# Fused attention kernel: computing 58 of 1184 softmax score banks with VectorE and GpSimd instead of ScalarE

## The chip, the cores and the metric

One NeuronCore of a Trainium2 chip runs the kernel. Times are device microseconds (us) of whole executions. Engines: PE (matmul), PEld (its weight loads), ACT (ScalarE), DVE (VectorE), POOL (GpSimd), SP (SyncE, here only a DMA queue). A ratio is the mean time of one kernel's fast runs over that of the kernel before in the same rounds, so it is not quite the ratio of the medians quoted beside it. One execution of the kernel before was slow (636 us, granted clock 0.655) and is in no ratio.

## The reference

Two attentions over 2048 tokens, model width 448, 16 heads of 28, bf16. Cut to what matters:

```python
# A: plain attention
scores = einsum('bhqd,bhkd->bhqk', q, k) * Dh ** -0.5
o = einsum('bhqk,bhkd->bhqd', softmax(scores), v)          # then @ wo
# B: four segments of 512: masked attention within a segment,
# mixed with a linear-attention memory of the earlier segments
o = g * (phi(qs) @ M) / (phi(qs) @ z + 1e-6) + (1 - g) * (softmax(logits + mask) @ vs)
M = M + phi(ks).T @ vs; z = z + phi(ks).sum()
```

## The kernel before

The work is cut into "banks" of 128 keys x 512 queries of one head. Three banks form a unit: PE writes its scores into one PSUM tile, and one ScalarE instruction takes the exp of all three. PE multiplies the weights with the values two units later. A "query block" is 512 queries of four heads of A (64 banks, 21.3 units). There are 16 of these; eight smaller "B blocks" are put between the later ones.

```python
ps = scp.tile([P, NB, CW], FP32, tag="sc", name="ps_s")        # two buffers of 3 banks
short = min(WARM - state["cols"] - P * nmask, 2 * CW) if u > 0 else 0
...                                                            # filler matmuls on `warm`
pt = ptp.tile([P, NB, CW], BF16, tag="pt", name="pt")
nc.scalar.activation(out=pt[:, 0:n, :], in_=ps[:, 0:n, :], func=ACT.Exp, scale=scale)
```

All other work (projections, outputs, B's memory) is "filler". PE does some columns of it in each unit. Every filler that multiplies writes one of the two PSUM buffers of the "ring" and DVE evicts it; the value accumulators `acc` use the same ring. When a query block ends, its denominators make a trip through DRAM, timed in units after the end:

```python
nc.vector.tensor_copy(out=o[:, 0, :], in_=a[:])                # evict acc
nc.sync.dma_start(out=d1..., in_=o[DH:P:HP, 0:planes, :])      # denominators out
at(u + 3, step1)    # SP:  load them back, spread over partitions
at(u + 7, step2)    # DVE: reciprocal;  SP: out again
at(u + 9, step3)    # SP:  load them broadcast
at(u + 14, step4)   # DVE: multiply
at(u + 16, step5)   # release the output projections as fillers
```

`loadB` (a filler) issues six weight loads and 16 transposing loads. At `nu - 2` (two units before the end) all fillers that are left run at once.

The softmax here doesn't subtract the row's maximum and nothing guards it: scores larger than these inputs give would overflow.

## Time and profile before

Median 581.53 us of 4 runs (580.49 to 585.9).

The page's busy table, then the page's costliest group. Columns of the group: line, engine, operation, output and input, shapes, count; busy us and mean ns of one; idle time of the engine just before them and what ended it.

```profile
PE 525.7 (91%) x3916; PEld 172.5 (30%) x3916; DVE 197.6 (34%) x388; ACT 548.7 (95%) x427; POOL 21.3 (4%) x41
...
L452 ACT ACTIVATE pt<-ps_s 128x1536 bf16<-128x1536 f32 x395 | 538.2, 1583 | 11.5 <-PE ps_s L439 5.9
```

The busy time of each engine between the start of the first exp and the end of the last (columns: stretch, its length, busy time of each engine with instruction counts, granted PE clock, DMA share, GB/s):

```profile
12.90:568.53 555.63, 510.80 (x3840) 165.22 (x3840) 191.60 (x370) 544.47 (x420) 14.45 (x27) 1.00 0.15 38
```

ScalarE idles for 555.63 - 544.47 = 11.2 us of that stretch. PE looks as busy, but 367 of its matmuls are filler on the warm tile. ScalarE is what bounds the kernel.

### The profile page before, as it was taken

To read this page: it belongs to the slowest core of one execution; us is meant where nothing else is said; L and a number is where in the kernel's file an instruction comes from. 1 tells how busy PE (TensorE), PEld (TensorE's weight loads), DVE (VectorE), ACT (ScalarE), POOL (GpSimd) and SP (SyncE) were. 2 spreads that over 40 slices of the span, in tenths; PEclk is the share of its full clock that TensorE was granted. 3 is DMA by queue.
4 is the path that set the end of the run, shared out by engine and by line. 5 is a ranking of instruction groups with operands and counts; after the bars stand their busy time and mean duration, and the time that the engine had idled before them with its cause. 6 is when DMAs were issued, how large, how long until landed. Compare 5 with 4: busy or idle time off the path is not lost.

```text
span 579.1 us, 9661 instructions
## 1 busy us (share of the span) xinstructions
PE 525.7 (91%) x3916; PEld 172.5 (30%) x3916; DVE 197.6 (34%) x388; ACT 548.7 (95%) x427; POOL 21.3 (4%) x41
## 2 busy tenths in 40 slices
PE   7999999999998998899899989989998998889985
PEld 3333322222232322332233322322322323323322
DVE  1232323222223323344434231324344354364212
ACT  3999999999999999999999999999999999999982
POOL 5700000000000000000000000000000000000000
PEclk9999999999999999999999999999999999999999
DMA  7600000001630000002002011021040121142101
GB/s 190 112 1 22 2 20 1 21 0 45 144 68 15 21 1 20 1 3 75 4 9 73 2 29 53 3 68 36 5 120 17 23 77 35 27 135 75 59 17 48
DMA packets 43571, 24.26 MB, mean 42 GB/s; under 512 B 31180, under 2 KB 37164, under 8 KB 43528
## 3 DMA queue, kind: packets, MB, share of 16 engines
q1 hardware_dynamic: 41784, 21.22, 14.5%
q10 hardware_dynamic: 1248, 1.53, 0.9%
q0 software_dynamic: 496, 0.91, 0.7%
q8 instruction: 30, 0.49, 0.4%
q14 instruction: 13, 0.11, 0.1%
HBM read 15.60 MB, written 4.37 MB: 34 GB/s over the span
## 4 chain that ended last, share of the span: by engine, by line
ACT 59%; PE 21%; issue 14%; DVE 3%; DMA 2%; SPq 0%; POOL 0%; ACTq 0%; DVEq 0%; POOLq 0%
ACT pt L452 56%; PE ps_s L439 5%; PE acc L484 4%; PE ps_proj L171 3%; PE ps_s L430 2%; PE ps_s L448 2%; PE ps_y L595 1%; ACT phq L508 1%; DMA w<-in_A_wqkv_dram 1%; ACT ek L691 1%; DVE y L603 1%; DVE osb L539 1%; PE ps_mem L520 1%; PE ps_v L199 1%; DMA bc<-d 0%
## 5 line engine op out<-in xcount | busy, mean ns | idle before, releaser
L452 ACT ACTIVATE pt<-ps_s 128x1536 bf16<-128x1536 f32 x395 | 538.2, 1583 | 11.5 <-PE ps_s L439 5.9
L439 PE MATMUL ps_s<-qTA,kTA 32*128 32x512 bf16 x1024 | 135.3, 384 | 2.1 <-ACT pt L452 1.5
L430 PE MATMUL ps_s<-warm,ident 128*128 128x512 bf16 (+6 forms) x367 | 101.7, 330 | 32.9 <-ACT pt L452 24.9
L484 PE MATMUL acc<-pt,vA 128*32 128x512 bf16 x1024 | 128.4, 390 | 0.2 <-DVE vA L188 0.2
L439 PEld LDWEIGHTS <-kTA 32*128 32x128 bf16 x1024 | 34.8, 90 | 143.5 <-issue 141.6
L484 PEld LDWEIGHTS <-vA 128*32 128x32 bf16 x1024 | 32.3, 92 | 70.7 <-issue 68.8
L430 PEld LDWEIGHTS <-ident 128*128 128x128 bf16 x367 | 35.3, 97 | 53.2 <-issue 43.7
L539 DVE COPY osb<-acc 128x512 f32<-128x512 f32 x32 | 22.1, 692 | 57.4 <-PE acc L484 57.1
L603 DVE CAST y<-ps_y 128x448 bf16<-128x448 f32 x28 | 17.5, 624 | 50.6 <-PE ps_y L595 50.6
L448 PE MATMUL ps_s<-tri,negi 128*128 128x128 bf16 x256 | 25.0, 222 | 0.0
L439 PE MATMUL ps_s<-qTB,kTB 32*128 32x384 bf16 (+3 forms) x256 | 24.5, 301 | 0.1
L176 DVE CAST kTA<-ps_proj 128x512 bf16<-128x512 f32 x15 | 10.4, 692 | 37.4 <-PE ps_proj L171 37.4
L176 DVE CAST qTA<-ps_proj 128x512 bf16<-128x512 f32 x15 | 10.4, 691 | 33.5 <-PE ps_proj L171 33.5
L171 PE MATMUL ps_proj<-xTB,wpqB 128*128 128x512 bf16 x64 | 20.7, 385 | 1.1 <-DVE macc L715 0.8
L171 PE MATMUL ps_proj<-xTB,wpkB 128*128 128x512 bf16 x64 | 20.6, 384 | 0.5
L204 DVE CAST vB<-ps_v 128x448 bf16<-128x448 f32 x16 | 9.9, 620 | 29.5 <-PE ps_v L199 29.5
L171 PE MATMUL ps_proj<-xTA,wpkA 128*128 128x512 bf16 x60 | 19.3, 384 | 0.5
L171 PE MATMUL ps_proj<-xTA,wpqA 128*128 128x512 bf16 x60 | 18.9, 384 | 0.8
L176 DVE CAST kTB<-ps_proj 128x512 bf16<-128x512 f32 x16 | 10.9, 684 | 24.1 <-PE ps_proj L171 24.1
L577 DVE TENSOR_TENSOR oT<-osb,bc 128x512 bf16<-128x512 f32 x19 | 13.1, 687 | 16.8 <-DMA bc<-d 16.7
L448 PEld LDWEIGHTS <-negi 128*128 128x128 bf16 x256 | 14.7, 97 | 13.5 <-issue 13.5
L199 PE MATMUL ps_v<-wstB,xTB 128*128 128x448 bf16 x64 | 18.7, 358 | 0.0
(118 smaller groups left out, 325.7 us busy)
## 6 DMA issues: line engine op xcount, KB each, us to landing
bc<-d SPq DMA_DIRECT2D x48, 128.0 KB
bc<-d SPq DMA_DIRECT2D x76, 64.0 KB
out_dram<-y SPq DMA_DIRECT2D x30, 112.0 KB
wstA<-in_A_wqkv_dram ACTq DMA_DIRECT2D x1, 1008.0 KB
xn<-in_A_x_dram SPq DMA_DIRECT2D x1, 448.0 KB
woA<-in_A_wo_dram POOLq DMA_DIRECT2D x4, 98.0 KB, 4.0
woB<-in_B_wo_dram POOLq DMA_DIRECT2D x4, 98.0 KB, 3.3
wstB<-in_B_wq_dram SPq DMA_DIRECT2D x1, 336.0 KB
```

The lines of the kernel that those rows point to most:

```text
L171: nc.tensor.matmul(ps[:], lhsT=wpad[which, side][:, c, g * P:(g + 1) * P], rhs=xc(side, sc, c)[:], start=(c == 0), stop=(c == NKC - 1))
L176: nc.vector.tensor_copy(out=dst[:], in_=ps[:])
L199: nc.tensor.matmul(ps[:, 0:n], lhsT=xc(side, t // 4, c)[:, (t % 4) * P:(t % 4 + 1) * P], rhs=w[side][:, c, 2 * D + h0 * DH:3 * D], start=( ...
L204: nc.vector.tensor_copy(out=v[side][:, t, h0 * HP:H * HP].rearrange("p (h e) -> p h e", e=HP)[:, :, 0:DH], in_=ps[:, 0:n].rearrange("p (h ...
L430: nc.tensor.matmul(ps[:, 0, 0:n], lhsT=ident[:], rhs=warm[:, 0:n], start=True, stop=True)
L439: nc.tensor.matmul(ps[:, i, o0:o0 + wd], lhsT=kT[side, g, t // 4][rows, (t % 4) * P:(t % 4 + 1) * P], rhs=qT[side, g, q0 // CW][rows, q0 % ...
L448: nc.tensor.matmul(ps[:, i, o0:o0 + P], lhsT=negi[:], rhs=tri[:], start=False, stop=True, skip_group_check=True)
L452: nc.scalar.activation(out=pt[:, 0:n, :], in_=ps[:, 0:n, :], func=ACT.Exp, scale=scale)
L484: nc.tensor.matmul(acc[key][j * HP:(j + 1) * HP, a0:a0 + wd], lhsT=v[side][:, t, h * HP:(h + 1) * HP], rhs=pt[:, i, c0:c0 + wd], start=fir ...
L539: nc.vector.tensor_copy(out=o[:, 0, :], in_=a[:])
L577: nc.vector.tensor_mul(oT[key][:], o[:, 0, :], bc[:, 0, :])
L603: nc.vector.tensor_copy(out=y[:], in_=ps)
```

## The change

Its intent is to take banks from ScalarE and give them to DVE and POOL, which have time. An offloaded bank has its own score matmul into a ring buffer. DVE turns scores into the 16-bit pattern of a bf16 power of two and splits it into mantissa `m` and exponent `y`; POOL evaluates `y * (m*m + PB)`. A second path, all on DVE ("V"), has a count of 0. The core of the diff, cut:

```diff
+OFF_V = 0
+OFF_Q = 4
-FILL = 820
-FILL_B = 760
+FILL = 1024
+FILL_B = 1024
-    w4p = ... bufs=7        otp = ... bufs=22      q tiles: bufs=15
+    w4p = ... bufs=6        otp = ... bufs=20      q tiles: bufs=13
-    w["0"] = ...            # three small first loads, of four heads' weights
-    load_w("0", ...)        # x3, then the whole weight load
+    load_w("A", A_wqkv, 0, 0, 3 * D, nc.scalar)   # the whole load at once
+    n = OFF_V + OFF_Q if p > 1 else 2             # banks off in query block p
+    rest = [b for b in banks if b not in off]     # 1126 banks, 376 units
+    def g_off(b):                                 # a filler, at most one in 4 units
+        nc.tensor.matmul(ps[:], lhsT=kT..., rhs=qT..., ...)          # ring buffer ps_x
+        nc.vector.tensor_scalar(out=y[:], in0=ps[:], ... op0=ALU.mult, op1=ALU.add)
+        # one unit later:
+        nc.vector.tensor_scalar(out=m[:], in0=y[:], scalar1=0x7F, scalar2=0x3F80, ...)
+        nc.vector.tensor_scalar(out=y[:], in0=y[:], scalar1=0x7F80, ...)
+        nc.gpsimd.tensor_tensor(out=t[:], in0=mf, in1=mf, op=ALU.mult)
+        nc.gpsimd.tensor_scalar(out=t[:], in0=t[:], scalar1=1.0, scalar2=PB, ...)
+        nc.gpsimd.tensor_tensor(out=pt[:], in0=t[:], in1=yf, op=ALU.mult)
+    # in loadB:
+        state["loaded"] = state["u"] + 14         # B's fillers wait for this unit
```

More of the change, by code (lines that the diff above doesn't have):

```diff
@@ L1 @@
+import math
 from contextlib import ExitStack
@@ L13 @@
 BF16 = mybir.dt.bfloat16
+U16 = mybir.dt.uint16
 FP32 = mybir.dt.float32
@@ L29 @@
 NEG = -16384.0
+PK = 0.33188195
+PA = -0.15702550544193214
+PB = 2.01442438
+PC = 23.0539507405541
+PD = 37.67976126880884
+LOG2E = 1.4426950408889634
+V_LAT = 9
+Q_LAT = 10
+OFF_V = 0
+OFF_Q = 4
 FILL_H = 1100
-FILL = 820
-FILL_B = 760
+FILL = 1024
+FILL_B = 1024
 WARM = 1050
@@ L68 @@
     big = ctx.enter_context(tc.tile_pool(name="big", bufs=1))
-    w4p = ctx.enter_context(tc.tile_pool(name="w4p", bufs=7))
+    w4p = ctx.enter_context(tc.tile_pool(name="w4p", bufs=6))
     w2p = ctx.enter_context(tc.tile_pool(name="w2p", bufs=3))
@@ L72 @@
     kqp = ctx.enter_context(tc.tile_pool(name="kqp", bufs=15))
-    otp = ctx.enter_context(tc.tile_pool(name="otp", bufs=22))
+    otp = ctx.enter_context(tc.tile_pool(name="otp", bufs=20))
     ptp = ctx.enter_context(tc.tile_pool(name="ptp", bufs=PT_BUFS))
@@ L77 @@
     rlp = ctx.enter_context(tc.tile_pool(name="rlp", bufs=1))
+    vxp = ctx.enter_context(tc.tile_pool(name="vxp", bufs=2))
+    vpp = ctx.enter_context(tc.tile_pool(name="vpp", bufs=3))
     ypool = ctx.enter_context(tc.tile_pool(name="ypool", bufs=4))
@@ L103, in w_tile @@
         w[side] = wts.tile([KC, NKC, 3 * D], BF16, tag="wst", name="wst" + side)
-        nc.gpsimd.memset(w[side][0:KC // 2, 3, :], 0.0)
+        nc.vector.memset(w[side][0:KC // 2, 3, :], 0.0)
     def load_w(side, src, c0, s0, n, eng):
@@ L114 @@
     w_tile("A")
-    w["0"] = wts.tile([KC, NKC, 3 * GW], BF16, tag="w0", name="w0")
-    nc.vector.memset(w["0"][0:KC // 2, 3, :], 0.0)
-    load_w("0", A_wqkv, GW, D, GW, nc.scalar)
-    load_w("0", A_wqkv, 0, 0, GW, nc.gpsimd)
-    load_w("0", A_wqkv, 2 * GW, 2 * D, GW, nc.sync)
+    load_w("A", A_wqkv, 0, 0, 3 * D, nc.scalar)
     warm = const.tile([P, CW], BF16)
@@ L125 @@
     nc.scalar.activation(out=dummy[:], in_=dummy[:], func=ACT.Exp)
-    load_w("A", A_wqkv, 0, 0, 3 * D, nc.scalar)
     ident = const.tile([P, P], BF16)
@@ L162, in kq_tile @@
     def kq_tile(which, side, g, sc):
-        t = kqp.tile([P, CW], BF16, tag=which, name=f"{which}T{side}")
+        t = kqp.tile([P, CW], BF16, tag=which, name=f"{which}T{side}", bufs=15 if which == "k" else 13)
         (kT if which == "k" else qT)[side, g, sc] = t
@@ L184, in g_v0 @@
                 nc.tensor.matmul(ps[:, t, :], lhsT=xc("A", r, c)[:, t * P:(t + 1) * P],
-                                 rhs=w["0"][:, c, 2 * GW:3 * GW], start=(c == 0), stop=(c == NKC - 1))
+                                 rhs=w["A"][:, c, 2 * D:2 * D + GW], start=(c == 0), stop=(c == NKC - 1))
             if t < 3:
@@ L239 @@
             xT["A", 0, 2 * half + i] = t
-    for i, which in enumerate(("q", "k")):
-        nc.vector.tensor_copy(
-            out=wpad[which, "A"][:].rearrange("k c (h e) -> k c h e", e=HP)[:, :, 0:4, 0:DH],
-            in_=w["0"][:, :, i * GW:(i + 1) * GW].rearrange("k c (h e) -> k c h e", e=DH))
+    pad_copy("k", "A", 0, 4)
+    pad_copy("q", "A", 0, 4)
     v = {}
@@ L340 @@
         banks += banks_A(2 + i // 4, i % 4)
-    units = [banks[i:i + NB] for i in range(0, len(banks), NB)]
-    per = 4 * NT * NCH // NB
+    off = {}
+    for p in range(1, 4 * NCH):
+        g, cq = p // 4, p % 4
+        n = OFF_V + OFF_Q if p > 1 else 2
+        for i in range(n):
+            off["A", g, cq, (2 * i + 1) * NT // (2 * n), (i + p) % 4] = (
+                "Q" if (i + 1) * OFF_Q // n > i * OFF_Q // n else "V")
+    rest = [b for b in banks if b not in off]
+    units = [rest[i:i + NB] for i in range(0, len(rest), NB)]
+    unit_of = {b: u for u, bs in enumerate(units) for b in bs}
+    off_at = {}
+    for p in range(1, 4 * NCH):
+        g, cq = p // 4, p % 4
+        us = [u for b, u in unit_of.items() if b[0:3] == ("A", g, cq)]
+        mine = [b for b in off if b[0:3] == ("A", g, cq)]
+        for i, b in enumerate(mine):
+            lat = V_LAT if off[b] == "V" else Q_LAT
+            lo, hi = min(us) + LAG - lat + 1, max(us) + LAG - 1 - lat
+            off_at.setdefault(max(lo + (2 * i + 1) * (hi - lo) // (2 * len(mine)), 24), []).append(b)
     nu = len(units)
@@ L362 @@
     urgent = deque()
-    state = {"u": 0, "hold": -1, "cur": None, "credit": 0.0, "cols": 0, "seq": 0, "fresh": False}
+    state = {"u": 0, "hold": -1, "cur": None, "credit": 0.0, "cols": 0, "seq": 0, "off": 0, "fresh": False}
     def at(u, fn):
@@ L384, in next_filler @@
         for n, (after, fn) in enumerate(misc):
-            if after <= state["u"]:
+            if (after() if callable(after) else after) <= state["u"]:
                 del misc[n]
@@ L405, in run_fillers @@
         while state["credit"] > 0:
-            if state["cur"] is None and not next_filler():
-                break
+            if state["cur"] is None:
+                if vq and state["u"] >= state["off"]:
+                    state["off"] = state["u"] + 4
+                    state["cur"] = g_off(vq.popleft())
+                elif not next_filler():
+                    break
             step_cur()
@@ L453, in emit_scores, with split, step, last @@
         return pt
+    def g_off(b):
+        kind, g, s, kt, j = b
+        rows = slice(j * HP, (j + 1) * HP)
+        ensure(("k", "A", g, kt // 4))
+        ensure(("q", "A", g, s))
+        ps = ring([P, CW], FP32, "ps_x")
+        nc.tensor.matmul(ps[:], lhsT=kT["A", g, kt // 4][rows, (kt % 4) * P:(kt % 4 + 1) * P],
+                         rhs=qT["A", g, s][rows, :], start=True, stop=True,
+                         tile_position=(j * HP, 0))
+        y = vxp.tile([P, CW], U16, tag="y", name="xy")
+        m = vxp.tile([P, CW], U16, tag="m", name="xm")
+        t = vxp.tile([P, CW], FP32, tag="t", name="xt", bufs=1)
+        mf, yf = m[:].bitcast(BF16), y[:].bitcast(BF16)
+        pt = vpp.tile([P, CW], BF16, tag="ptv", name="ptv")
+        u = state["u"]
+        nc.vector.tensor_scalar(out=y[:], in0=ps[:], scalar1=scale * LOG2E * 2.0 ** 7,
+                                scalar2=(127.0 + math.log2(PK)) * 2.0 ** 7, op0=ALU.mult, op1=ALU.add)
+        def split():
+            nc.vector.tensor_scalar(out=m[:], in0=y[:], scalar1=0x7F, scalar2=0x3F80,
+                                    op0=ALU.bitwise_and, op1=ALU.bitwise_or)
+            nc.vector.tensor_scalar(out=y[:], in0=y[:], scalar1=0x7F80, scalar2=None,
+                                    op0=ALU.bitwise_and)
+            if off[b] == "Q":
+                pool()
+        def step(src, c):
+            nc.vector.scalar_tensor_tensor(out=t[:], in0=src, scalar=c, in1=mf,
+                                           op0=ALU.add, op1=ALU.mult)
+        def last():
+            nc.vector.scalar_tensor_tensor(out=pt[:], in0=t[:], scalar=PD, in1=yf,
+                                           op0=ALU.add, op1=ALU.mult)
+            vpend.append((b, pt, state["u"] + 1))
+        def pool():
+            nc.gpsimd.tensor_tensor(out=t[:], in0=mf, in1=mf, op=ALU.mult)
+            nc.gpsimd.tensor_scalar(out=t[:], in0=t[:], scalar1=1.0, scalar2=PB,
+                                    op0=ALU.mult, op1=ALU.add)
+            nc.gpsimd.tensor_tensor(out=pt[:], in0=t[:], in1=yf, op=ALU.mult)
+            vpend.append((b, pt, u + Q_LAT - 4))
+        at(u + 1, split)
+        if off[b] == "V":
+            at(u + 2, lambda: step(mf, PA))
+            at(u + 2, lambda: step(t[:], PB))
+            at(u + 3, lambda: step(t[:], PC))
+            at(u + 3, last)
+        yield -CW
     def pv_parts(b):
@@ L469 @@
     acc_left = {}
+    opened = set()
     for b in banks:
@@ L472 @@
             acc_left[p_[0]] = acc_left.get(p_[0], 0) + 1
+            acc_left[p_[0], b[4]] = acc_left.get((p_[0], b[4]), 0) + 1
+    vpend = deque()
+    vq = deque()
     held_z = {}
@@ L483, in emit_pv_part @@
         h = 4 * b[1] + j
+        if side == "A":
+            acc_left[key, j] -= 1
+            first, last = (key, j) not in opened, acc_left[key, j] == 0
+            opened.add((key, j))
         nc.tensor.matmul(
@@ L486, in emit_pv_part @@
             lhsT=v[side][:, t, h * HP:(h + 1) * HP],
-            rhs=pt[:, i, c0:c0 + wd],
+            rhs=pt[:, c0:c0 + wd] if i is None else pt[:, i, c0:c0 + wd],
             start=first, stop=last, tile_position=(0, j * HP), skip_group_check=True)
@@ L738 @@
     first_u = {}
-    for n, b in enumerate(banks):
+    for b in banks:
         if b[0] != "A":
-            first_u.setdefault((b[1], b[2] // 2), n // NB)
+            first_u.setdefault((b[1], b[2] // 2), unit_of[b])
     blocks = list(first_u)
@@ L747, in add_kqB @@
             for s in (2 * sp, 2 * sp + 1):
-                add(g_kq, which, "B", g, s, after=first_u[blocks[min(n - 1, 5)]] if n else 0)
+                add(g_kq, which, "B", g, s, after=first_u[blocks[min(n - 1, 5)]] if n else lambda: state.get("loaded", 10 ** 6))
     for s in range(NSEG):
         for t in range(4):
-            add(g_v, "B", 4 * s + t, 0)
+            add(g_v, "B", 4 * s + t, 0, after=lambda: state.get("loaded", 10 ** 6))
         if s == 0:
-            add(padB)
+            add(padB, after=lambda: state.get("loaded", 10 ** 6))
         if s >= 1:
-            add(g_m, s - 1)
+            add(g_m, s - 1, after=lambda: state.get("loaded", 10 ** 6))
         if s == 1:
@@ L761 @@
             for t in range(4):
-                add(g_kn, s, t)
+                add(g_kn, s, t, after=lambda: state.get("loaded", 10 ** 6))
     for n in range(4, 8):
@@ L818 @@
         run_pv(NB + 1)
+        while vpend and vpend[0][2] <= u and acc.get(("A",) + vpend[0][0][1:3]) is not None:
+            b, ptv, _ = vpend.popleft()
+            emit_pv_part(b, None, ptv, pv_parts(b)[0])
+        vq.extend(off_at.get(u, ()))
         for e in sorted(x for x in events if x[0] <= u):
@@ L823 @@
     finish_cur()
+    assert not vpend and not vq
     assert not pend and not events and not misc and not held_z and not urgent
```

## The prediction

> **What bounds it now.** ScalarE. The page's busy table has ACT at 548.7 us of a 579.1 us span (95%), and the chain of waits gives it 59%, nearly all in the softmax exp. The groups show 395 exps of 128x1536 taking 538.2 us: 1.36 us each, 0.454 us per 512-column bank; in the timeline they start 1.33 us apart. The first starts at 12.9 us, the last ends at 568.5 us, and waits before exps are only about 11 us. PE shows 91%, but 367 of its matmuls (101.7 us) are filler on the warm tile; when catching up it needs 1.20 us a unit, so it has 0.13 us of slack in each. DVE is 34% busy, POOL 4%.
>
> **What the change does.** It takes 58 of the 1184 score banks off ScalarE. For each, DVE scales PSUM scores into 16-bit bits (one op), splits mantissa and exponent (two 16-bit ops) and POOL evaluates a quadratic (three ops). (The all-DVE path "V" has a count of 0.) Exp units fall from 395 to 376.
>
> Gain: 58 x 0.454 = 26.3 us of ScalarE, all of it critical.
>
> Costs, per bank:
> - DVE: a 128x512 PSUM eviction takes 0.69 us here; the two 16-bit tensor_scalar ops should be like the 128x512 bf16 one in this trace, 0.285 us (the Trainium skill's "VectorE: DVE Perf Modes", perf-mode tier table, gives that class the fourfold mode). Together 1.26 us, 73 us in all: DVE goes to about 270 us, 48%.
> - POOL: no such op in this trace. The Trainium skill's "GPSIMD Engine Reference" (Elementwise, side by side) has a two-input op at 4497 ns for 2048 elements; estimate 1.1 us at 512, and 0.5 to 0.8 us for the one-input op: about 3 us a bank, 175 us in all. The schedule leaves six units (8 us), less 1.6 us for the DVE part, so PE should not wait for it.
> - PE: a lone score and a lone value matmul, 0.21 us each, where in threes they cost 0.11; part of it displaces warm filler.
> - Ring: 58 more users of the two small PSUM buffers, so fillers wait more for DVE evictions. Exp waits grow from 11 to some 14 to 18 us.
> - Start: the small first weight load goes, and the first padding waits for the whole 1.2 MB. The small load landed at 9.2 us with the large one competing. At the 340 to 390 GB/s seen at 5 to 8 us, both large loads (1.6 MB) should land by 8 to 10 us. First exp at 13 us, give or take 1.
> - End: four output projections in a row rather than three, about 1 us. One large work buffer fewer (6 for 7) may add 1 to 2 us where two B blocks follow each other.
>
> Sum: 581.5 - 26.3 + about 4 = 559 us.
>
> **Prediction.** 559 us, eight times in ten between 552 and 568. Faster by over 2%: 0.87; within 2%: 0.11; slower: 0.02.
>
> **What would show it.** Right: 376 exps of unchanged 1.36 us, ACT busy near 522 us, exp waits under 18 us, DVE near 270 us, POOL near 200 us, PE clock above 0.98, first exp near 13 us. Wrong: exp starts over 1.34 us apart for long stretches; value matmuls of offloaded banks waiting for POOL; PE waiting for DVE in the ring; first exp after 15 us.
>
> **What would make it wrong.** POOL ops far slower than estimated (above 6 us a bank PE stalls in order, and everything behind it); POOL and DVE slowing one another at SBUF, which lengthens evictions; bitwise ops at 0.69 us; a weight load that lands much later, so that the start eats the gain.

## The result, and the profile after

Median 571.99 us of 10 runs (569.8 to 574.21) against 581.14; ratio 0.9834, 95% interval 0.9811 to 0.9857. The gain is 9 us, where 22 were predicted. The same lines of the changed kernel (page, then the stretch from first to last exp):

```profile
PE 526.1 (92%) x3861; PEld 173.7 (30%) x3861; DVE 284.8 (50%) x563; ACT 525.8 (92%) x408; POOL 189.1 (33%) x211
...
L480 ACT ACTIVATE pt<-ps_s 128x1536 bf16<-128x1536 f32 x376 | 513.1, 1490 | 26.4 <-PE ps_s L467 19.5
...
11.72:559.83 548.11, 511.64 (x3784) 166.75 (x3783) 278.45 (x545) 521.57 (x401) 185.09 (x200) 0.99 0.16 39
```

ScalarE's work fell by 548.7 - 525.8 = 22.9 us, the start came 1.2 us earlier, and the idle time between the exps rose from 11.2 to 548.11 - 521.57 = 26.5 us. -22.9 - 1.2 + 15.4 = -8.7 us, which is the difference of the two spans (579.1 and 570.4). So the work left ScalarE as planned, and ScalarE then waited. Where (idle us of ScalarE in the timeline, gaps summed by stretch):

| stretch | before | after |
|---|---|---|
| start (to 30 us) | 0 | 1.0 |
| load of B's inputs (160 to 175 us) | 0.2 | 4.9 |
| normalisation after two B blocks in a row (500 to 540 us) | 2.0 | 6.6 |
| last output projections (550 to 563 us) | 3.4 | 4.8 |
| all else, mostly (5.4 and 6.4 us) at the masked units of the B blocks, where extra matmuls add the mask | 5.6 | 9.2 |

**The gap at 164 us.** Timeline of the kernel before, the queue SP and then DVE (start, duration, engine, line, operation; in brackets the idle time before and what ended it; the view's window cuts off the earlier of the 16 transposes), and the PE instruction that next needed the ring:

```profile
155.01 11.98 SPq L99 DMA_TRANSPOSE xTB<-in_B_x_dram  x9
167.09 0.54 SPq L545 DMA_DIRECT2D d<-osb  x1
...
166.38 0.62 DVE L204 CAST vB<-ps_v 128x448 bf16<-128x448 f32 x1 [3.35 <-PE ps_v L199]
170.60 0.25 DVE L558 RECIPROCAL r<-r 128x16 f32<-128x16 f32 x1 [3.60 <-DMA r<-d]
170.77 0.56 DVE L204 CAST vB<-ps_v 128x448 bf16<-128x448 f32 x1
...
171.53 0.74 PE L686 MATMUL ps_kn<-wstB,xTB 128*128 128x448 bf16 x3
```

The same place in the changed kernel: SP, DVE, then PE, and ScalarE's next exp.

```profile
150.45 11.22 SPq L113 DMA_TRANSPOSE xTB<-in_B_x_dram  x8
161.76 0.55 SPq L631 DMA_DIRECT2D d<-osb  x1
...
165.29 0.25 DVE L644 RECIPROCAL r<-r 128x16 f32<-128x16 f32 x1 [4.25 <-DMA r<-d]
...
165.93 0.62 DVE L213 CAST vB<-ps_v 128x448 bf16<-128x448 f32 x1
...
161.14 0.93 PE L208 MATMUL ps_v<-wstB,xTB 128*128 128x448 bf16 x4
...
166.60 0.91 PE L208 MATMUL ps_v<-wstB,xTB 128*128 128x448 bf16 x2 [3.67 <-DVE vB L213]
...
168.53 1.45 ACT L480 ACTIVATE pt<-ps_s 128x1536 bf16<-128x1536 f32 x1 [4.54 <-PE ps_s L467]
```

Both kernels have the late transfer: the denominators wait for the transposes on the SP queue, and DVE sits 3.6 and 4.3 us at the reciprocal. In the kernel before one eviction stood behind it too (170.77), but PE came to its next projection only at 171.53 and did not wait. In the changed kernel the eviction of `ps_v` (written by 162.1) stands behind the reciprocal, the next projection needs that buffer, and the scores stand behind the projection in PE's order. The Trainium skill ("TensorE: Matmul & The Clock Gate", Architectural detail, queue depths) calls DVE's queue a strict FIFO (first in, first out); this trace agrees: the eviction, ready at 162.1, ran at 165.93, behind the reciprocal of 165.29.

PE then ran at half its clock for a while. The windows view of the changed kernel, around this gap and around one at 508 us (the clock is the third number from the end):

```profile
166.30:169.60 3.30, 3.00 (x11) 0.75 (x11) 0.36 (x2) 1.07 (x1) 2.89 (x5) 0.50 0.24 74
507.70:514.30 6.60, 5.73 (x24) 1.18 (x22) 3.52 (x10) 3.56 (x3) 2.86 (x3) 0.50 0.55 144
```

The same page (Part 1) says that an idle window of about 3.4 us brings the half rate, and that activity ends it. The first of these follows an idle time of 3.67 us. The second follows no idle time as long in the timeline: in the 3.4 us before it PE was busy for 1.81 us, and its one wait there took 1.66 us (a wait of 0.87 us lies inside the stretch). Between its exps the kernel before has no half rate.

**The gaps after 503 us.** Changed kernel, POOL, then DVE, then PE:

```profile
501.33 1.67 POOL L520 TENSOR_SCALAR xt<-xt 128x512 f32<-128x512 f32 x1
503.08 1.47 POOL L522 TENSOR_TENSOR ptv<-xt,xy 128x512 bf16<-128x512 f32 x1
...
501.30 1.22 DVE L665 TENSOR_TENSOR osb<-osb,bc 128x1024 f32<-128x1024 f32 x1
...
503.46 1.12 DVE L643 TENSOR_SCALAR r<-r 128x16 f32<-128x16 f32 x1
...
505.11 0.62 DVE L689 CAST y<-ps_y 128x448 bf16<-128x448 f32 x1
...
505.78 0.37 PE L489 MATMUL ps_x<-qTA,kTA 32*128 32x512 bf16 x1 [1.66 <-DVE y L689]
```

A DVE operation on 16 columns takes 1.12 us and ends with POOL's operation (503.46 + 1.12 = 504.58; 503.08 + 1.47 = 504.55). Before that POOL's one-input operation (0.62 us where nothing disturbs it) took 1.67 us beside DVE's two-input one. The eviction of `ps_y` comes late, and the score matmul of an offloaded bank, itself in the ring, waits 1.66 us with all scores behind it.

**The end.** A query block now has 20 units instead of 21.3. The last block but one releases its four output projections 16 units after an end that lies two units into the last block: that is just the unit where all leftover fillers are flushed. Four run in a row (three before), each waiting for an eviction. PE of the changed kernel:

```profile
551.66 0.93 PE L681 MATMUL ps_y<-woA,oT 128*128 128x448 bf16 x4
553.30 0.92 PE L681 MATMUL ps_y<-woA,oT 128*128 128x448 bf16 x4 [0.71 <-DVE y L689]
554.94 0.92 PE L681 MATMUL ps_y<-woA,oT 128*128 128x448 bf16 x4 [0.72 <-DVE y L689]
556.57 0.92 PE L681 MATMUL ps_y<-woA,oT 128*128 128x448 bf16 x4 [0.72 <-DVE y L689]
557.42 0.39 PE L467 MATMUL ps_s<-qTA,kTA 32*128 32x512 bf16 x3
```

### The profile page after: what moved, and what is told of

Same layout as the page of the kernel before. It is cut to its first block, busy times and chain, and to the rows that moved or that the text cites. A ratio compares the mean times of both kernels' runs of the same rounds, so it can differ in the third digit from the quotient of the medians.

```text
span 570.4 us, 10019 instructions
## 1 busy us (share of the span) xinstructions
PE 526.1 (92%) x3861; PEld 173.7 (30%) x3861; DVE 284.8 (50%) x563; ACT 525.8 (92%) x408; POOL 189.1 (33%) x211
## 4 chain that ended last, share of the span: by engine, by line
PE 40%; ACT 38%; DVE 8%; issue 8%; SPq 3%; DMA 3%; ACTq 0%; DVEq 0%
ACT pt L480 36%; PE ps_s L467 9%; PE acc L570 8%; PE ps_proj L180 8%; PE ps_s L458 4%; PE ps_y L681 3%; SPq L113 3%; PE ps_v L208 2%; PE ps_s L476 2%; PE ps_x L489 2%; DVE y L689 1%; DMA xn<-in_A_x_dram 1%; ACT phq L594 1%; DMA xTA<-in_A_x_dram 1%; DVE osb L665 1%
## 5 line engine op out<-in xcount | busy, mean ns | idle before, releaser
L480 ACT ACTIVATE pt<-ps_s 128x1536 bf16<-128x1536 f32 x376 | 513.1, 1490 | 26.4 <-PE ps_s L467 19.5
L519 POOL TENSOR_TENSOR xt<-xm 128x512 f32<-128x512 bf16 x58 | 62.7, 1082 | 336.7 <-DVE xm L502 336.7
L458 PE MATMUL ps_s<-warm,ident 128*128 128x512 bf16 (+6 forms) x312 | 94.1, 357 | 16.3 <-ACT pt L480 12.1
L522 POOL TENSOR_TENSOR ptv<-xt,xy 128x512 bf16<-128x512 f32 x58 | 68.5, 1181 | 4.8
L498 DVE TENSOR_SCALAR xy<-ps_x 128x512 uint16<-128x512 f32 x58 | 40.0, 690 | 48.8 <-PE ps_x L489 48.7
L458 PEld LDWEIGHTS <-ident 128*128 128x128 bf16 x312 | 28.3, 97 | 58.9 <-issue 53.3
L520 POOL TENSOR_SCALAR xt<-xt 128x512 f32<-128x512 f32 x58 | 40.4, 697 | 5.1
L489 PE MATMUL ps_x<-qTA,kTA 32*128 32x512 bf16 x58 | 22.1, 381 | 3.7 <-DVE y L689 1.9
L467 PE MATMUL ps_s<-qTB,kTB 32*128 32x512 bf16 (+3 forms) x256 | 23.1, 300 | 0.2
L570 PE MATMUL acc<-ptv,vA 128*32 128x512 bf16 x58 | 22.3, 385 | 0.0
```

The source lines that it names most:

```text
L458: nc.tensor.matmul(ps[:, 0, 0:n], lhsT=ident[:], rhs=warm[:, 0:n], start=True, stop=True)
L467: nc.tensor.matmul(ps[:, i, o0:o0 + wd], lhsT=kT[side, g, t // 4][rows, (t % 4) * P:(t % 4 + 1) * P], rhs=qT[side, g, q0 // CW][rows, q0 % ...
L489: nc.tensor.matmul(ps[:], lhsT=kT["A", g, kt // 4][rows, (kt % 4) * P:(kt % 4 + 1) * P], rhs=qT["A", g, s][rows, :], start=True, stop=True ...
L498: nc.vector.tensor_scalar(out=y[:], in0=ps[:], scalar1=scale * LOG2E * 2.0 ** 7, scalar2=(127.0 + math.log2(PK)) * 2.0 ** 7, op0=ALU.mult, ...
L519: nc.gpsimd.tensor_tensor(out=t[:], in0=mf, in1=mf, op=ALU.mult)
L520: nc.gpsimd.tensor_scalar(out=t[:], in0=t[:], scalar1=1.0, scalar2=PB, op0=ALU.mult, op1=ALU.add)
```

## The experiments

Theory (queue): the gain was given back at a few places, each with its own cause, where something that waits stands ahead of the scores in an engine's order. Rival 1 (contention): POOL and DVE slow one another throughout, and that ate the gain. Rival 2: the other parts of the change (filler rates, fewer buffers, the new start) did. All kernels ran 3 rounds on top of the profiled run; all gave correct results but the one marked.

| run | median us | ratio, 95% interval |
|---|---|---|
| changed kernel | 571.99 | 0.9834 (0.9811 to 0.9857) |
| e1_split_load | 568.01 | 0.9769 (0.9737 to 0.9801) |
| e2_no_pool (wrong) | 567.87 | 0.9758 (0.9719 to 0.9798) |
| e4_no_offload | 582.21 | 1.0012 (0.9979 to 1.0045) |
| e5_early_last | 567.46 | 0.9751 (0.9716 to 0.9786) |
| e6_split_early | 563.50 | 0.9688 (0.9665 to 0.9711) |
| e7_less_at_end | 562.04 | 0.9667 (0.9643 to 0.9691) |
| e8_late_steps | 567.05 | 0.9757 (0.9722 to 0.9793) |
| e9_x_first | 560.98 | 0.9653 (0.9635 to 0.9670) |
| e10_all | 559.81 | 0.9631 (0.9602 to 0.9660) |
| e11_more5 | 559.62 | 0.9631 (0.9584 to 0.9678) |
| e12_before_early | 577.67 | 0.9940 (0.9905 to 0.9975) |
| e13_slow_fill | 572.34 | 0.9832 (0.9793 to 0.9872) |

### e1_split_load

```diff
-        for r in range(4):
+        for r in range(2):
             for c in range(NKC):
                 load_xT("B", Bx, r, c, nc.sync)
-        state["loaded"] = state["u"] + 14
+        state["loaded"] = state["u"] + 11
+        state["load2"] = state["u"] + 26     # then a second filler loads r = 2, 3
```

> The changed kernel, with the load of B's inputs issued in two halves (weights and 8 transposes, then 8 transposes 26 units later), so that the SP queue is free when a block's denominators have to go out. Queue theory (DVE works in order; a reciprocal that waits for a late transfer holds up the PSUM evictions behind it, PE stalls on the ring, its clock is throttled, and ScalarE starves): the exp gap of about 4.7 us near 162 us and the half-clock window near 166 us go, the time falls by 4 to 6 us, to about 567. Contention theory (POOL and DVE slow one another everywhere and that is what ate the gain): the time stays within 1.5 us of the changed kernel's 572.

Measured: 568.01 us. The denominators go out at 152.6 us instead of 161.8, and both the gap at 164 us and the half clock after it are gone from the profile. The queue theory holds for this gap; it is worth 4.0 us.

### e8_late_steps

```diff
+        late = 4 if key == ("A", 1, 0) else 0     # the one block behind the load
-        at(u + 7, step2)
+        at(u + 7 + late, step2)                   # same for step3, step4, step5
```

> The changed kernel with its one B load, unsplit and on the same queue; only the four later normalisation steps of the one query block whose denominators go out behind that load are emitted 4 units later. The transfers are as late as before, but DVE comes to the waiting reciprocal after three more PSUM evictions. If DVE's order is what turns a late transfer into a stall: the gap near 164 us goes and the time falls by about 4 us, to 568. If the traffic of the load itself slows PE or ScalarE there: no change, 572.

Measured: 567.05 us, and no exp gap between 150 and 200 us. DVE's timeline in this run:

```profile
165.09 0.62 DVE L213 CAST vB<-ps_v 128x448 bf16<-128x448 f32 x1 [0.41 <-PE ps_v L208]
167.57 0.62 DVE L213 CAST vB<-ps_v 128x448 bf16<-128x448 f32 x1 [1.85 <-PE ps_v L208]
169.34 0.62 DVE L213 CAST vB<-ps_v 128x448 bf16<-128x448 f32 x1 [1.15 <-PE ps_v L208]
169.88 0.24 DVE L644 RECIPROCAL r<-r 128x16 f32<-128x16 f32 x1
```

The load is untouched and the traffic the same. Moving one group of instructions back in DVE's order is enough. So the traffic is not the cause; the order is. (e1 also moved the gate of B's fillers from 14 to 11 units, so e8 is the cleaner test. Its profile is of the slowest of the four runs, 570.1 us: it also shows an exp gap of 1.9 us at 21 us, larger than in the other runs.)

### e13_slow_fill

```diff
-        run_fillers(FILL_H if u < 22 ...
+        run_fillers(760 if 100 < u < 126 else FILL_H if u < 22 ...
```

> The changed kernel with the filler rate put back to the 760 columns of the kernel before, but only in units 101 to 125, around the late denominators near 162 us. The transfers stay as late and DVE's order around the waiting reciprocal stays the same; PE only comes later to the projection that needs the blocked PSUM buffer. If the faster rate is part of the cause there: the gap of 4.5 us near 164 us shrinks to under 2.5 us and 2 to 4 us come back (568 to 570). If DVE's order alone decides: no change, 572.

Measured: 572.34 us. The gap was 3.3 us with 0.6 us behind it (4.5 and 0.3 in the changed kernel), and small gaps turned up elsewhere. Nothing came back: the faster filler rate is not what made this gap.

### e2_no_pool

```diff
-            nc.vector.tensor_scalar(out=y[:], in0=y[:], scalar1=0x7F80, ...)
-            if off[b] == "Q": pool()
+            nc.vector.tensor_scalar(out=pt[:].bitcast(U16), in0=y[:], scalar1=0xFFFF, ...)
+            vpend.append((b, pt, u + Q_LAT - 4))
```

> The changed kernel, but the three POOL operations of each offloaded bank are left out: the third DVE operation writes the unmasked 16-bit word as the weight (wrong by up to a few per cent in those banks, on purpose). DVE has as many operations as in the changed kernel, PE and the queues too. Contention theory: DVE operations return to their old durations (denominator scalar op 168 ns for 430, tensor multiply 687 ns for 881) and most of the missing 13 us comes back: 563 or less. Queue theory: the durations return too, but only 1 to 4 us come back (568 to 571), and the gap near 162 us stays.

Measured: 567.87 us, result wrong. Two groups of DVE's operations in the kernel before, the changed kernel and this run, one fence each (busy us, mean ns of one):

```profile
L577 DVE TENSOR_TENSOR oT<-osb,bc 128x512 bf16<-128x512 f32 x19 | 13.1, 687 | 16.8 <-DMA bc<-d 16.7
L557 DVE TENSOR_SCALAR r<-r 128x16 f32<-128x16 f32 x12 | 2.0, 168 | 1.5 <-DMA r<-d 1.5
```

```profile
L663 DVE TENSOR_TENSOR oT<-osb,bc 128x512 bf16<-128x512 f32 x19 | 16.7, 881 | 7.2 <-DMA bc<-d 7.0
L643 DVE TENSOR_SCALAR r<-r 128x16 f32<-128x16 f32 x12 | 5.2, 430 | 0.0
```

```profile
L662 DVE TENSOR_TENSOR oT<-osb,bc 128x512 bf16<-128x512 f32 x19 | 13.0, 683 | 9.2 <-DMA bc<-d 9.2
L642 DVE TENSOR_SCALAR r<-r 128x16 f32<-128x16 f32 x12 | 2.0, 167 | 0.0
```

The contention is real. The Trainium skill ("GPSIMD Engine Reference", Key points) says that POOL shares its SBUF interfaces with DVE; these lines agree and give sizes. Its price in time is 4.1 us of the missing 13, at the edge of what the queue theory allowed. Most of it lies after 500 us, where the idle time falls from 6.6 to 3.3 us. The gap near 164 us stays (4.0 us), so contention is not its cause.

### e4_no_offload

```diff
-        n = OFF_V + OFF_Q if p > 1 else 2
+        n = 0
-    add(loadB)
+    add(loadB, after=98)
```

> The changed kernel with no bank offloaded (395 exps again), all else of the change kept: start, buffers, filler rates, gates; the load of B's inputs is held to unit 98, where the kernel before has it. It says what the rest of the change is worth by itself. If the offload alone brought the waits: first exp 1.2 us earlier, exp waits near the 11 us of before, about 580 us. If the faster filler rate or the fewer buffers brought them: 583 to 592 us, with exp waits of 15 us and more.

Measured: 582.21 us. First exp 0.9 us earlier than before, exp idle 13.6 us against 11.2, of which 2.0 us at 21 to 26 us where PE waits for late input tiles. The faster filler rate and the fewer buffers by themselves are nearly free, so rival 2 falls as a cause on its own; whether they cost something beside the offload was tried only for the rate at one gap (e13). The new start gains nothing: what the first exp wins is lost ten microseconds later. Against this run the offload is worth 582.21 - 571.99 = 10.2 us.

### e5_early_last and e6_split_early

```diff
+        fast = key == ("A", G - 1, NCH - 2)
-        at(u + 3, step1)   # 7, 9, 14, 16 for the others
+        at(u + (2 if fast else 3), step1)   # 4, 6, 10, 11
```

> The changed kernel, with the normalisation steps of the last query block but one placed at units 2, 4, 6, 10, 11 after its end in place of 3, 7, 9, 14, 16, so that its four output projections run as filler instead of all at once before the last two exps. Both theories: the exp gap of 5.0 us near 552 us goes (under 0.7 us), time about 567 to 568; a smaller gain would mean that the projections disturb the exps where they now run.

Measured: 567.46 us, 4.5 us gained; the gap near 553 us is gone.

> Both mends together: the load of B's inputs in two halves and the early normalisation of the last query block but one. If the two gaps are separate, their gains add: 571.99 less 4.0 less 4.5, about 563.5 us; if ScalarE's gaps only move elsewhere, 566 or more.

Measured: 563.50 us. The two gains add (4.0 + 4.5; measured 8.5), so these gaps were separate losses.

### e7_less_at_end

On top of e6. The block meant in the expectation is the last but one, the one that follows two B blocks in a row.

```diff
-        n = OFF_V + OFF_Q if p > 1 else 2
+        n = (0 if p == 14 else OFF_V + OFF_Q) if p > 1 else 2
```

> As the run with both mends, but the four offloaded banks of the third last query block but one (the one that follows two B blocks in a row) go back to ScalarE, so that DVE and POOL have nothing of the offload where four B heads are normalised. Costs 4 x 0.444 = 1.8 us of ScalarE. Queue theory: the exp idle of about 6 us between 500 and 525 us shrinks to the 1.8 us that the kernel before had there, and the half-clock window near 508 us goes: 2 to 3 us faster than the run with both mends, about 561. If the offload is not the cause there: 1.8 us slower than it.

Measured: 562.04 us, against 563.50 for e6. The idle time after 500 us falls from 5.2 to 2.3 us and the half clock there is gone, although ScalarE has four banks more. The gain (1.5 us) is below the 2 to 3 us expected, and the intervals of the two runs overlap, so only the mechanism is shown, by the profile, and not the size.

### e9_x_first

On top of e6. The whole weight load goes behind the first input tile on the SP queue:

```diff
-    load_w("A", A_wqkv, 0, 0, 3 * D, nc.scalar)
+    load_w("A", A_wqkv, 0, 0, 3 * D, nc.sync)
```

> As the run with both mends, but the first weight load is issued on the SP queue, behind the first input tile, and not beside it on the ACT queue. The input tile should land about 2 us earlier (4.7 us in the kernel before, 7.0 us in the changed one), the 12 transposes start earlier, and the two exp gaps near 23 and 27 us (1.0 us together) go; first exp at 11 to 12 us. 1 to 1.5 us faster than the run with both mends, about 562. If the weights land later for it, the first exp comes later and nothing is gained.

Measured: 560.98 us. The input tile is used at 4.0 us (7.0 in the changed kernel), the first exp starts at 11.4 us, and there is no idle time between exps before 30 us. The profile of e6 has only 0.1 us there without this edit, so this pair does not show the gain; but the nine profiles with the changed start have 0.1 to 3.6 us there, and the three with this edit (e9, e10, e11) none. The 2.5 us against e6 are not explained in full; the intervals of the two overlap a little.

### e10_all and e11_more5

e10 is e9 with the edit of e7. e11 also has `OFF_Q = 5` and one offloaded bank in 3 units at the earliest.

> All four mends: B load in halves, early normalisation of the last query block but one, input tile ahead of the weights, no offload in the query block after the two B blocks. Gains add again: 560.98 less 1.5, about 559.5 us, exp idle about 13 us.

> All four mends and five offloaded banks per block in place of four (67 in all for 54, one g_off every 3 units at the earliest). 13 x 0.444 = 5.8 us of ScalarE. If what is left of the exp idle is not the offload's doing: about 554 us. If each offloaded bank costs a share of its gain in waits (in the changed kernel 10 of 26 us arrived): 557 to 558 us.

Measured: 559.81 us and 559.62 us. The page of e10, and its stretch from first to last exp:

```profile
PE 516.5 (92%) x3814; PEld 173.7 (31%) x3857; DVE 278.8 (50%) x551; ACT 527.6 (94%) x409; POOL 176.1 (31%) x199
...
11.72:548.67 536.95, 501.56 (x3738) 166.20 (x3782) 272.51 (x533) 523.34 (x402) 172.12 (x188) 1.00 0.16 40
```

Idle: 536.95 - 523.34 = 13.6 us, with all of the offload but four banks still there. e10 is the version that beats both kernels, by 12 us the changed one. The fifth bank per block of e11 bought nothing: in the profile ScalarE's work between the exps fell by only 3.4 us (523.34 to 519.93) of the 5.8 expected, and its idle time rose by 3.7 us, most of it in one new gap of 3.0 us at 194 us. What stands in the way there was not looked into.

### e12_before_early

The edit of e5 on the kernel before.

> The kernel before, with no offload, and only the early normalisation of the last query block but one. The exp gap of 3.4 us near 563 us goes: 578 us. It says how much of the mended kernels' gain the kernel before could have had without the change.

Measured: 577.67 us. So some 3.5 us (1.5 to 5.5 by the interval) of the mended kernels' gain has nothing to do with the offload. From 577.67 to 559.81 are 17.9 us, for 54 banks that take 24.0 us of ScalarE (54 x 0.444). Two of the other mends were not tried on the kernel before.

## Why the prediction was wrong

It said 559 us (552 to 568) and 0.87 for faster by over 2%; the measured time is 571.99, faster by 1.7%.

- "ScalarE bounds it; exp units fall from 395 to 376": right.
- "Gain: 58 x 0.454 = 26.3 us, all of it critical": too large by 3.4 us. ScalarE's busy time fell by 22.9 us. An exp alone takes 1.45 us, but in a row they start 1.33 us apart, so each stop costs some 0.12 us more. The changed kernel has 40 stops between its exps and the kernel before 18; that would make 2.6 us (an estimate from these numbers).
- "Exp waits grow from 11 to some 14 to 18 us": this is the step that failed. They became 26.5 us. I had added up the work of DVE and POOL and found room on both, and had not asked what stands ahead of what. The term of 4 us in the sum for waits, end and buffers measured 15.4 us: 4.7 at the B load (shown by e1 and e8), 4.6 after 500 us (contention and ring; e2 and e7), 1.4 at the end (the gap shown by e5), 1.0 at the start (it varies between profiles; see e9), and 3.6 spread over the rest: 1.0 of it at the masked units of the B blocks (5.4 to 6.4), the others in scattered waits of under 0.9 us. These last were not tested and stay open.
- The end: "about 1 us" more for a fourth projection in a row was right (1.4), but removing the whole burst was worth 4.5 us.
- "One large work buffer fewer may add 1 to 2 us": not seen. e4 has the fewer buffers and 1.1 us of idle between 500 and 540 us, less than the 2.0 of the kernel before.
- "First exp at 13 us": it came at 11.7. The loss that I feared there appeared later, in the transposed input tiles, which start at 7.1 us for 4.9 because the first tile shares the DMA engines with the weights.
- DVE at about 270 us: 284.8; the three operations cost what was said (0.690, 0.286 and 0.294 us), the rest is contention: e2, with as many DVE operations and none of the offload's on POOL, has 264.0. POOL: 1.08, 0.70 and 1.18 us, about 3 us a bank as estimated. "PE should not wait for POOL": right, no value matmul of an offloaded bank shows such a wait.
- "PE waiting for DVE in the ring" was named among the signs of being wrong; that is the sign that came.

What stays open: why the first B projection falls just behind the waiting reciprocal in this kernel. In the kernel before several projections had been evicted ahead of the reciprocal, and the new gate, which holds B's fillers until the load is due, makes them later. But the gate alone is not enough: e4 keeps it and has only 0.2 us of idle there. In e4 the first projection starts 5.3 us after the block's `acc` is evicted (165.12 against 159.85), and two evictions come ahead of the reciprocal (169.02), which does not wait; in the changed kernel it starts 9.2 us after (161.14 against 151.90). So it seems to be where the gate opens against the block's end, which the shorter blocks moved; no run changes that alone.

## What to carry to other kernels

Moving work from the bound engine to idle ones gains what was moved only if nothing in the receiving engine's order waits ahead of what the bound engine needs; read the receiving engine's timeline around each transfer that it waits for, and not its busy share. Steps timed in units (here 16 units after a block's end) can change places when the units per block change, so look at the flush at the end again. Several small gaps with separate causes can be mended one at a time, and here the gains added: 4.0, 4.5, 2.5 and about 1.2 us (the last two within overlapping intervals).

## What the Trainium skill lacked or had wrong

- "GPSIMD Engine Reference", Key points, names the contention with DVE but gives no size (the page "SBUF — State Buffer" treats the sharing at more length, but not for these operations). Here a 16-column DVE operation (0.17 us alone) took 1.12 us and ended with POOL's operation; DVE's two-input multiply went from 687 to 881 ns on average, and POOL's one-input operation from 0.62 to 1.67 us beside it. Evictions from PSUM stayed at 692 ns.
- The table of "GPSIMD Engine Reference" has times for a two-input operation on 2048 fp32 elements only. At 512 elements the runs show 1.08 us (bf16 in, fp32 out), 1.16 us undisturbed (fp32 and bf16 in, bf16 out), and 0.62 us for a one-input operation.
- "ScalarE: Activation LUTs", What ACT_TABLE_LOAD costs, has back-to-back instructions overlap by about 93 ns. Here exps of 128x1536 from PSUM take 1.45 us alone and start 1.33 us apart, an overlap of about 0.12 us.
- "TensorE: Matmul & The Clock Gate", Part 1, has one idle window of about 3.4 us as the condition for the half rate, and frequent short idle times as a second way to it, for which it gives no size. Near 508 us the half rate came (6.6 us of it) after 3.4 us in which PE was busy for 1.81 us and waited at most 1.66 us at once; in e4 it came at 23.7 us after 3.4 us with 1.92 us busy and no wait over 0.9 us.
